# Turning x on the vector engine by block transposes, and splitting the third pair's output projection over idle stretches of the tail

## The chip, the cores and the metric

One Trainium2 chip, one core. The metric is the device time of one execution in microseconds (us). Beside it stands the span of the core, mostly about 1.2 us shorter, which a profile covers. Engines: PE is TensorE (matmul), PEld its weight load, DVE is VectorE, ACT is ScalarE, POOL is GpSimd, SP is SyncE, which here only issues DMA transfers.

## The reference

Two independent problems, A and B, of the same form: one decoding step of attention over a sliding window of a cache. Cut to what matters:

```
# B=2, Sq=1, D=576, Hq=32, Hkv=16, Sk=16384, Dh=128, W=4096, bf16
q = (x @ wq).reshape(B, 1, Hq, Dh)           # x [2,1,576], wq [576,4096]
k, v = k_cache[:, :, -W:], v_cache[:, :, -W:] # each K/V head serves two query heads
p = softmax(q k^T * Dh**-0.5);  o = p v
out = o.reshape(B, 1, Hq*Dh) @ wo             # wo [4096,576]
result = concatenate([A, B], axis=-1)
```

Of the 153 MB that must be read, 134 are K and V. They come as 16 K tiles and 16 V tiles of 4096 KB each, into a ring of four slots; wq (4608 KB per problem) passes through the same ring first.

## The kernel before

The parts that the change and the argument touch; `# ...` marks cuts. Each operation carries its list of dependencies; the order of operations on each engine is the order of the calls. Of the helpers, make_PV multiplies with one V tile, make_evac brings the product out of PSUM, make_dg and make_pick bring it into the form that the output projection reads, and make_projm and make_proj are output projections, with the weight wo.

```python
# The SP queue: wq A, wq B, then the K and V tiles in order.
# wq fills slots 0, 1 and a quarter of slot 2; the first K tile goes to slot 3, the second to slot 0.
slot_of[key] = (n_slot + 3) % NSLOT
first_deps = {0: [q_done[0]], 1: [q_done[0], q_done[1]], 2: [q_done[1]], 3: []}
deps = [last_reader[prior[-1]]] if prior else first_deps[r]     # of the DMA of a tile
# ...
# x: masked copy on DVE, nine PE transposes, two ACT copies, then the projections
d_xs = dve(lambda e: e.tensor_tensor(xs8.rearrange("p (i t) -> p i t", t=2),
                 x8[:, :].unsqueeze(2).broadcast_to([8, D, 2]),
                 hmask[:, 0:2].unsqueeze(1).broadcast_to([8, D, 2]), ALU.mult), [x_dma, d_hm], "xs8")
def f_xT(e, bank):
    bb = bank[:].bitcast(BF16)
    for u in range(NU):                                          # NU = 9
        src = xs8.rearrange("b (c t) -> b t c", t=NU)[:, u, :]
        last = e.transpose(bb[:, 8 * u:8 * u + 8], src, ident_b[0:8, 0:8])
    return last
# ...
q_done[P] = pe(f_q, [wq_dma[P], op_xev], "q%d" % P)              # 36 matmuls for each problem
# ...
# the tail
make_PV(i + 1); make_evac(i + 1)
make_projm(NM - 1)                    # the third pair's projection, 16 steps of two matmuls
make_part(); make_dg(NG - 2); make_pick(NG - 2)
make_rsum(NG - 1); make_pT(NG - 1); make_sums(NG - 1)
make_PV(i + 2); make_evac(i + 2)
make_PV(i + 3, (0,)); make_dg(NG - 1, (0,)); make_pick(NG - 1, (0,))
filler(2)                             # matmuls whose result nobody reads, for the PE clock
make_PV(i + 3, (1, 2)); make_evac(i + 3)
filler(2)
make_dg(NG - 1, (1,)); make_pick(NG - 1, (1,))
make_proj(NG - 2); make_proj(NG - 1); make_E(NPROB - 1)
```

## Time and profile before

| | before |
|---|---|
| time, median of the first 3 runs | 363.27 us (363.23 to 363.83) |
| span of the profiled run | 362.4 us |
| bytes on the one busy DMA queue | 153.1 MB |
| share of the 16 DMA engines' time | 98.5% |

The page of the kernel before, its DMA row in 40 slices (tenths busy) and the queue's line (packets, MB, share of the engines' span):

```profile
span 362.4 us, 2626 instructions
...
DMA  8999999999999999999999999999999999999995
...
q1 hardware_dynamic: 6196, 153.10, 98.5%
```

The DMA engines are busy from the second slice to the last but one. So the kernel's time is the time of the stream, plus a start, plus what follows the last landing.

The timeline of the kernel before between the landing of x and the first projection matmul (columns: start us, duration us, engine, line, operation, tiles, count, and in brackets the idle time before and what ended it):

```profile
15.52 1.35 DVE L217 TENSOR_TENSOR pR<-tmp,hmask 8x1152 bf16<-8x1152 bf16 x1 [13.96 <-DMA tmp<-in_B_x_dram]
...
16.93 0.70 PE L258 MATMUL tb<-ident_b,pR 8*128 8x8 bf16 x9 [16.93 <-DVE pR L217]
...
17.66 0.29 ACT L265 ACTIVATE pT<-tb 128x36 bf16<-128x36 bf16 x2 [12.60 <-PE tb L258]
...
18.09 0.59 PE L279 MATMUL ot<-ring,pT 128*32 128x512 bf16 x1 [0.47 <-ACT pT L265]
```

x lands at 15.5 us and the projection starts at 18.09. The SP engine's DMA issues of the kernel before, from 25 us (the first line merges three K tiles, the second to the fourth; the second K tile's issue is its start):

```profile
27.96 8.95 SPq L377 DMA_DIRECT2D ring<-in_A_k_cache_dram  x3
44.03 0.54 SPq L377 DMA_DIRECT2D ring<-in_A_v_cache_dram  x1
56.13 0.53 SPq L377 DMA_DIRECT2D ring<-in_A_k_cache_dram  x1
```

The second K tile waits for projection A, which reads its slot; it goes out at 27.96 us. The first K tile was issued at 1.73 and took 33.5 us, so it landed at 35.2.

The stretches of the kernel before (stretch and length, busy us of PE, PEld, DVE, ACT, POOL, then granted PE clock, DMA share, GB/s):

```profile
28.00:34.00 6.00, 6.00 (x29) 0.68 (x7) 0.00 (x0) 0.00 (x0) 0.00 (x0) 1.00 1.00 431
34.00:40.00 6.00, 2.70 (x16) 0.67 (x9) 4.77 (x2) 3.00 (x9) 0.00 (x0) 0.92 1.00 431
350.00:356.00 6.00, 4.91 (x29) 1.04 (x20) 1.80 (x4) 0.00 (x0) 0.00 (x0) 0.50 1.00 416
356.00:360.00 4.00, 3.57 (x28) 2.08 (x30) 1.02 (x4) 0.00 (x0) 0.00 (x0) 0.51 0.64 249
```

The stream keeps 431 GB/s through 28 to 40 us. At the end the PE runs at half its clock (granted 0.50 and 0.51 in the last two stretches). The PE's timeline of the tail before:

```profile
352.88 1.90 PE L535 MATMUL ot<-ring,pT 128*32 128x512 bf16 x16 [0.62 <-DMA ring<-in_B_v_cache_dram]
...
357.16 3.45 PE L635 MATMUL pj<-wob,oP 128*2 128x288 bf16 x32
```

The last projection runs 32 matmuls in 3.45 us without a pause and ends at 360.61; the output transfer follows.

### The profile page before, as it was taken

What the parts mean: (1) busy time and instruction counts of PE and PEld (TensorE: products, weight loads), DVE (VectorE), ACT (ScalarE), POOL (GpSimd) and SP (SyncE); (2) the same over time, 40 slices, a digit from 0 to 9 for tenths busy, and PEclk for the clock granted to TensorE, in tenths of its full rate; (3) what the DMA queues carried; (4) which work ended last, traced back from release to release, by engine and by line L of the source; (5) the groups of instructions that cost most, each with busy time, mean ns of one, the idle gap of its engine ahead of it and who ended that gap; (6) DMA issues with size and microseconds to landing.
All of it is one profiled execution on the core that took longest, in us unless ns stands there. A gap on an engine that the chain in (4) does not pass through costs nothing.

```text
span 362.4 us, 2626 instructions
## 1 busy us (share of the span) xinstructions
PE 238.9 (66%) x1294; PEld 58.3 (16%) x935; DVE 211.4 (58%) x141; ACT 46.3 (13%) x80; POOL 22.3 (6%) x83
## 2 busy tenths in 40 slices
PE   0099599556666847662596677557686875666657
PEld 0010111112111201110121121112112120112222
DVE  0201879495949391934909476582917685765532
ACT  1000300040031000400005000500005000501300
POOL 3000101100010001000010000100010001001000
PEclk9999699969897896888888686998688798879976
DMA  8999999999999999999999999999999999999995
GB/s 326 452 427 416 448 418 441 427 430 438 416 447 416 452 416 420 448 423 442 423 436 430 427 434 418 437 441 416 438 429 432 434 434 431 435 423 438 412 415 233
DMA packets 6228, 153.28 MB, mean 423 GB/s; under 512 B 700, under 2 KB 840, under 8 KB 1224
## 3 DMA queue, kind: packets, MB, share of 16 engines
q1 hardware_dynamic: 6196, 153.10, 98.5%
q8 instruction: 9, 0.15, 0.2%
q14 instruction: 3, 0.02, 0.0%
q10 hardware_dynamic: 20, 0.01, 0.0%
HBM read 153.10 MB, written 0.00 MB: 422 GB/s over the span
## 4 chain that ended last, share of the span: by engine, by line
DVE 36%; DMA 28%; PE 23%; issue 8%; ACT 2%; POOL 1%; ACTq 0%; SPq 0%; DVEq 0%; POOLq 0%
DVE xt L432 23%; DMA ring<-in_B_k_cache_dram 16%; DMA ring<-in_B_v_cache_dram 8%; PE st L248 8%; PE st L458 7%; PE pj L248 3%; DMA tmp<-in_B_x_dram 3%; DVE pT L505 3%; DVE oR L564 3%; DVE mx L466 2%; DVE tmp L557 2%; ACT pR L496 1%; PE ot L279 1%; PE pj L616 1%; PE pj L635 1%
## 5 line engine op out<-in xcount | busy, mean ns | idle before, releaser
L458 PE MATMUL st<-xt,zq 128*128 128x512 bf16 x256 | 123.8, 484 | 82.8 <-DVE xt L432 81.4
L432 DVE STREAM_TRANSPOSE xt<-ring 128x4096 f32<-128x4096 f32 x32 | 141.4, 4426 | 27.6 <-DMA ring<-in_A_k_cache_dram 17.0
L248 PE MATMUL st<-xt,zq 128*128 128x512 bf16 x256 | 122.5, 478 | 0.0
L496 ACT ACTIVATE pR<-st,bias 128x512 bf16<-128x512 f32 x32 | 40.1, 1423 | 219.4 <-DVE bias L489 219.4
L458 PEld LDWEIGHTS st<-xt,zq 128*128 128x128 bf16 x256 | 29.3, 114 | 207.0 <-issue 109.4
L535 PE MATMUL ot<-ring,pT 128*32 128x512 bf16 x512 | 32.0, 392 | 8.1 <-DMA ring<-in_B_v_cache_dram 5.6
L489 DVE SCALAR_TENSOR_TENSOR bias<-vmask,tb,offm 128x4 f32<-128x4 f32 x8 | 1.8, 224 | 40.3 <-PE tb L486 40.3
L519 DVE TENSOR_REDUCE ssum<-tb 128x2 f32<-128x8 f32 x8 | 1.3, 161 | 37.4 <-PE tb L516 37.4
L424 POOL TENSOR_TENSOR zq<-qs,bmask 128x64 bf16<-128x64 bf16 x32 | 8.7, 294 | 168.0 <-PE st L248 146.3
L505 DVE STREAM_TRANSPOSE pT<-pR 128x2048 bf16<-128x2048 bf16 x8 | 18.4, 2304 | 0.7 <-ACT pR L496 0.7
L535 PEld LDWEIGHTS ot<-ring,pT 128*32 128x32 bf16 x512 | 12.3, 97 | 22.9 <-DMA ring<-in_B_v_cache_dram 10.6
L557 DVE SCALAR_TENSOR_TENSOR tmp<-ot,rsb,dmask 128x512 f32<-128x512 f32 x16 | 11.5, 718 | 7.7 <-PE ot L535 7.6
L564 DVE TENSOR_REDUCE oR<-tmp 128x128 f32<-128x512 f32 x15 | 15.6, 1043 | 0.5
L248 PE MATMUL pj<-wob,oM 128*2 128x288 bf16 x48 | 11.9, 286 | 0.0
L616 PE MATMUL pj<-wob,oM 128*2 128x288 bf16 x48 | 11.9, 286 | 0.0
L258 PE MATMUL tb<-ident_b,pR 8*128 8x8 bf16 x9 | 0.7, 198 | 16.9 <-DVE pR L217 16.9
L248 PE MATMUL pj<-ring,pT 128*32 128x512 bf16 x36 | 11.7, 409 | 0.0
L466 DVE TENSOR_REDUCE mx<-st 128x2 f32<-128x1024 f32 x8 | 9.7, 1213 | 0.1
L217 DVE TENSOR_TENSOR pR<-tmp,hmask 8x1152 bf16<-8x1152 bf16 x1 | 1.3, 1347 | 14.0 <-DMA tmp<-in_B_x_dram 14.0
L496 ACT ACTIVATION_READ_ACCUMULATOR pR<-st,bias 128x1 f32 x32 | 9.1, 286 | 0.0
L279 PE MATMUL ot<-ring,pT 128*32 128x512 bf16 x18 | 7.5, 419 | 0.5 <-ACT pT L265 0.5
L248 PE MATMUL st<-ring,pT 128*32 128x512 bf16 x18 | 7.3, 407 | 0.0
(69 smaller groups left out, 71.5 us busy)
## 6 DMA issues: line engine op xcount, KB each, us to landing
ring<-in_A_k_cache_dram SPq DMA_DIRECT2D x8, 4096.0 KB, 24.5
ring<-in_A_v_cache_dram SPq DMA_DIRECT2D x8, 4096.0 KB, 29.6
ring<-in_B_k_cache_dram SPq DMA_DIRECT2D x8, 4096.0 KB, 26.6
ring<-in_B_v_cache_dram SPq DMA_DIRECT2D x7, 4096.0 KB, 28.8
ring<-in_A_wq_dram SPq DMA_DIRECT2D x1, 4608.0 KB, 13.8
ring<-in_B_wq_dram SPq DMA_DIRECT2D x1, 4608.0 KB, 24.2
wob<-in_A_wo_dram SPq DMA_DIRECT2D x2, 2304.0 KB, 28.8
wob<-in_B_wo_dram SPq DMA_DIRECT2D x1, 2304.0 KB, 27.5
```

The costliest lines, as they stand in the source:

```text
L248: return e.add_instruction(mybir.InstMatmult(name=nc.get_next_instruction_name(), engine=mybir.EngineType.PE, ins=[e.lower_ap(mv_), e.lowe ...
L279: last = e.matmul(QB[c], wt, mv_, start=first, stop=True, skip_group_check=True)
L424: last = e.tensor_tensor(dst, src, msk, ALU.mult)
L432: Xop[(t, jh)] = dve(lambda e: e.transpose(xt[:, jh, :].bitcast(FP32).rearrange("p (kp x kt) -> p x kp kt", kp=2, kt=2), ring[:, r, jh * H ...
L458: last = e.matmul(ob, wt, mv_, start=first, stop=True, skip_group_check=True)
L466: ch[(G, "max")] = dve(lambda e: e.tensor_reduce(mx[:], st[:, :].rearrange("p (x t) -> p t x", t=2), AX.X, ALU.max), [Sop[(2 * G + 1, 1)]] ...
L496: last = e.activation(pR[:].rearrange("p (x k) -> p k x", k=4)[:, kv, :], st[:, :].rearrange("p (x t) -> p t x", t=2)[:, kv % 2, :], ACTF.Exp,
L505: pT_op[G] = dve(lambda e: e.transpose(pT[:, v, :].rearrange("p (w j q) -> p j w q", w=4, q=8), pR[:].rearrange("p (j w q) -> p j w q", w= ...
L535: last = e.matmul(OTB[32 * c:32 * c + 32, :], pT[:, v, base + 32 * c:base + 32 * c + 32], ring[:, r, jj * 128:(jj + 4) * 128], start=rd == ...
L557: evac_op[i] = dve(lambda e: e.scalar_tensor_tensor(tv, o, rsb[:, v, b:b + 1], dm, ALU.mult, ALU.mult), deps, "ev%d" % i)
L564: ch[(G, "red%d" % b)] = dve(lambda e: e.tensor_reduce(oR[:, b, :], tmp[:].rearrange("p (j d) -> p d j", j=4), AX.X, ALU.add), [evac_op[i] ...
L616: last = e.matmul(PJ[h], oM[:, j, :], mv_, start=start and j == 0, stop=True, skip_group_check=True)
```

## The change

Two independent parts. In the head, x is spread over 32 partitions and turned by eight block transposes on DVE, which takes PE, a PSUM bank and ACT out of the path. In the tail, the third pair's projection is cut in three, with the last four steps and a filler set behind the next-to-last V product, the fillers are longer, and the transfer of the first of the last two wo halves depends only on the projection's first part. The core of the diff, with cuts marked:

```diff
-        x8 = tmp[0:8, 0:D // 2].bitcast(BF16)
-        xs8 = pR[0:8, 0:2 * D]
+        xz = xt[0:32, 0, 0:NPROB * D]
+        xs = xt[0:32, 1, 0:NPROB * 2 * D]
 # ... xz is zeroed by POOL, x is loaded into xz, hmask grows to 32 partitions
+        d_xs = dve(lambda e: e.tensor_tensor(xs.rearrange("p (i t) -> p i t", t=2),
+                                             xz.unsqueeze(2).broadcast_to([32, NPROB * D, 2]),
+                                             hmask[:, 0:2].unsqueeze(1).broadcast_to([32, NPROB * D, 2]), ALU.mult), [x_dma, d_hm], "xs")
+        def f_xT(e):
+            for P in range(NPROB):
+                for k in range(4):
+                    last = e.transpose(xU[32 * k:32 * k + 32, P, :, :],
+                                       xs[:, P * 2 * D:(P + 1) * 2 * D].rearrange("p (c t) -> p t c", t=NU)[:, :, 32 * k:32 * k + 32])
+            return last
 # ... the nine PE transposes and two ACT copies are gone
-            q_done[P] = pe(f_q, [wq_dma[P], op_xev], "q%d" % P)
+            q_done[P] = pe(f_q, [wq_dma[P], d_xT], "q%d" % P)
 # ... tail
-        make_projm(NM - 1)
-        make_part()
+        make_projm(NM - 1, 0, 8)
         make_dg(NG - 2)
+        make_projm(NM - 1, 8, 12)
         make_pick(NG - 2)
 # ...
         make_PV(i + 2)
+        make_projm(NM - 1, 12, 16)
+        filler(4)
+        make_part()
         make_evac(i + 2)
 # ...
-        filler(2)
+        filler(4)
         make_PV(i + 3, (1, 2))
         make_evac(i + 3)
-        filler(2)
+        filler(3)
```

More of the change, by code (lines that the diff above doesn't have):

```diff
@@ L120, in build_kernel @@
         bsel = sb("bsel", [128, 2], FP32)
-        hmask = sb("hmask", [8, 2], FP32)
+        hmask = sb("hmask", [32, 2], FP32)
         mx = sb("mx", [128, 2], FP32)
@@ L178, in f_x @@
                 for h in range(2):
-                    last = e.dma_start(x8[4 * P + 2 * h:4 * P + 2 * h + 2, :], probs[P][0][:, 0, :]).then_inc(x_sem, 16)
+                    last = e.dma_start(xz[4 * P + 2 * h:4 * P + 2 * h + 2, P * D:(P + 1) * D], probs[P][0][:, 0, :]).then_inc(x_sem, 16)
             return last
@@ L199, in build_kernel @@
                                                    base=0, channel_multiplier=1), [p_ones_b], "ident_b")
-        p_zxU = pool(lambda e: e.memset(pTf[:, 0:XW].bitcast(FP32), 0.0), [], "zero_xU")
-        x_dma = dma_op("act", x_sem, 2 * NPROB, f_x, [p_zxU], "x")
+        p_zx = pool(lambda e: e.memset(xz.bitcast(FP32), 0.0), [], "zero_x")
+        x_dma = dma_op("act", x_sem, 2 * NPROB, f_x, [p_zx], "x")
         def f_sel(e):
@@ L215, in mask @@
             return dve(lambda e: e.tensor_reduce(dst, view, axes, ALU.add), [p_ident_f], tag)
-        d_hm = mask(hmask[:, 0:2], ident_f[0:8, 0:8].rearrange("p (g t b) -> p t g b", g=2, t=2), AX.XY, "hmask")
-        d_xs = dve(lambda e: e.tensor_tensor(xs8.rearrange("p (i t) -> p i t", t=2),
-                                             x8[:, :].unsqueeze(2).broadcast_to([8, D, 2]),
-                                             hmask[:, 0:2].unsqueeze(1).broadcast_to([8, D, 2]), ALU.mult), [x_dma, d_hm], "xs8")
+        d_hm = mask(hmask[:, 0:2], ident_f[0:32, 0:32].rearrange("p (g t b) -> p t g b", g=8, t=2), AX.XY, "hmask")
+        d_xs = dve(lambda e: e.tensor_tensor(xs.rearrange("p (i t) -> p i t", t=2),
[7 more added lines that the diff above has]
+            return last
+        d_xT = dve(f_xT, [d_xs], "xT")
         d_bm = mask(bmask[:, 0:4], ident_f[:].rearrange("p (a i) -> p a i", a=4), AX.X, "bmask")
@@ L252, in mm_held @@
                 tile_size=size, tile_position=at))
-        def f_xT(e, bank):
-            bb = bank[:].bitcast(BF16)
-            for u in range(NU):
-                src = xs8.rearrange("b (c t) -> b t c", t=NU)[:, u, :]
-                last = e.transpose(bb[:, 8 * u:8 * u + 8], src, ident_b[0:8, 0:8])
-            return last
-        n_, bank_x, op_xT = tb_job(f_xT, "xT", [d_xs, p_ident_b])
-        def f_xev(e):
-            for P in range(NPROB):
-                src = bank_x[:].bitcast(BF16)[:, 0:NU * 8].rearrange("c (u w) -> c u w", u=NU)[:, :, 4 * P:4 * P + 4]
-                last = e.activation(xU[:, P, :, 4 * P:4 * P + 4], src, ACTF.Copy)
-            return last
-        op_xev = act(f_xev, [op_xT, p_zxU], "xev")
-        tb_consumer[n_] = op_xev
         q_done = {}
@@ L344, in build_kernel @@
         projm_op = {}
+        projm_first = {}
         def issue(key):
@@ L353, in issue @@
                 rows = probs[P][4][gl * 1024:gl * 1024 + 128 * n, :].rearrange("(p j) n -> p j n", j=n)
-                deps = ([projm_op[i - 1]] if i >= 1 else []) if kind == "M" else [projm_op[NM - 1]]
+                deps = ([projm_op[i - 1]] if i >= 1 else []) if kind == "M" else [projm_first[NM - 1] if i == NG - 2 else projm_op[NM - 1]]
                 cuts = [(0, n, wo_sem[i % 2])]
@@ L430, in make_X @@
             r = slot_of[("K", t)]
-            deps = [stream_dma[("K", t)][0][2], Sop[(t - 1, jh)] if t >= 1 else op_xT]
+            deps = [stream_dma[("K", t)][0][2], Sop[(t - 1, jh)] if t >= 1 else d_xT]
             Xop[(t, jh)] = dve(lambda e: e.transpose(
@@ L499, in f @@
                 return last
-            exp_op[G] = act(f, [b4] + prev(G, "rsum8") + ([pT_op[G - 1]] if G >= 1 else [op_xT]), "exp%d" % G)
+            exp_op[G] = act(f, [b4] + prev(G, "rsum8") + ([pT_op[G - 1]] if G >= 1 else []), "exp%d" % G)
         def make_pT(G):
@@ L555, in make_evac @@
             deps = [PVop[i], d_dm, rsb_op[G]]
-            deps.append(ch["tmp"] if i else d_xs)
+            if i:
+                deps.append(ch["tmp"])
             evac_op[i] = dve(lambda e: e.scalar_tensor_tensor(tv, o, rsb[:, v, b:b + 1], dm, ALU.mult, ALU.mult), deps, "ev%d" % i)
@@ L603, in make_pick, with make_projm @@
             ch["tmp"] = ch[(G, "oP", b0)]
-        def make_projm(q):
-            P, start = 2 * q // GP, (2 * q) % GP == 0
+        def make_projm(q, j0=0, j1=16):
+            P, start = 2 * q // GP, (2 * q) % GP == 0 and j0 == 0
             ensure(("M", q))
             def f(e):
-                for j in range(16):
+                for j in range(j0, j1):
                     for h in range(2):
@@ L620, in make_projm @@
                 deps += [e_ops[(P - 1, 0)], e_ops[(P - 1, 1)]] if P >= 1 else [q_ev[2]]
-            projm_op[q] = pe(f, deps, "projm%d" % q)
+            projm_op[q] = pe(f, deps, "projm%d_%d" % (q, j0))
+            if j0 == 0:
+                projm_first[q] = projm_op[q]
         def make_proj(G):
```

## The prediction

> **What bounds the kernel now.** The DMA stream. The page shows one hardware queue with 153.1 MB at 98.5% of the DMA engines' time, in a span of 362.4 us; in the stretches table no 20 us between 40 and 340 us fall below 0.98 of DMA share. Only about 2 us at the start, and what follows the last landing, lie outside. The queue's issue list shows why compute delays between cost nothing: a K or V transfer takes about 10 us, but lands 24 to 31 us after issue, so two to three are queued.
>
> **Head.** x lands at 15.5 us (timeline). Before: masked copy on DVE 1.35 us (8x1152), nine PE transposes 0.7 us, two ACT copies 0.3 us; the first projection matmul starts at 18.09. After: the copy doubles to 2304 elements per partition, 2.7 us; then eight block transposes of 288 elements. The 2048-element bf16 transpose took 2304 ns, so I estimate 0.32 to 0.36 us each, 2.6 to 2.9 us together. The larger memset holds the x DMA back 0.3 us. The first projection matmul starts near 21.4, some 3.3 us later: a loss on the compute chain. The second K tile is issued when projection A ends, 27.9 before, about 31.3 after; the first K tile lands at 35.2, so the queue should not run dry, though the margin shrinks from 7 to 4 us. Tiles 3 and 4 go out at 39 instead of 35.7, with the second landing near 45. Later issues move 3 us, with 10 or more us queued. Cost to the end: 0, at worst 1 us.
>
> **Tail.** The last V piece arrives near 354.1; the two last wo halves land at 356.9 (first) and 358.4, 359.4, 359.9 (three cuts; issue plus time to landing). The granted PE clock is 0.50 from about 350 to 359.8, after PE sat idle 2.8 us before 349.2. The last projection ran without a gap, 32 matmuls in 3.45 us from 357.16, ending 360.6. The change moves four of sixteen projection steps (about 1 us) and a filler of four behind the next-to-last V product (346.4), so that the idle stretch shrinks to about 1 us, and lengthens the later fillers. [...] At full clock the projection takes about 1.9 us and then waits for wo, ending near 360.2. The earlier pick and second transpose (about 1.9 us earlier) gain nothing: the V tile they wait with lands at 344.4. Issuing the first wo half earlier, the second later (about 348), gains nothing: both stand behind V in the queue until 353. Gain: 0.3 to 0.6 us.
>
> **Time.** 363.27 - 0.45 + 0.15 = 363.0 us; 8 in 10: 362.4 to 364.0. Faster by over 2%: 0.01; within 2%: 0.98; slower by over 2%: 0.01.
>
> **What would show it.** Masked copy 2.6 to 2.8 us, eight transposes near 0.35 us each, first projection matmul near 21.4; DMA share unchanged between 20 and 60 us; next-to-last V product still starting at 344.4; granted clock 1.0 from 349 on; waits on wo inside the last projection; its end near 360.2.
>
> **What would make it wrong.** DMA share dropping near 31 to 36 us (the queue ran dry, up to 2 us); cold fillers delaying the last V products past their landing; the longer idle before 344.4 (about 4 us, as projection steps moved away) making that product and its followers late; the late issue of the second wo half moving its landing.

That a shorter idle stretch and longer fillers would keep the clock full was the estimate, from this one trace (granted clock 0.50 after 2.8 us of idle).

## The result, and the profile after

| | before | after |
|---|---|---|
| time, median of 6 runs | 363.74 us (363.23 to 364.07) | 365.01 us (364.77 to 365.61) |
| ratio, 95% interval | | 1.004 (1.0027 to 1.0053) |
| span of the profiled run | 362.4 us | 363.5 us |
| first projection matmul | 18.09 us | 24.10 us |
| second K tile issued | 27.96 us | 33.43 us |

A ratio is the mean time of one kernel's runs over that of the other's of the same rounds, so it is not quite the ratio of the medians. The change costs 1.3 us by the medians (1.5 by the ratio), clear of the noise, where a small gain was forecast and 364.0 was the upper bound.

The timeline of the changed kernel over the same path:

```profile
15.79 2.54 DVE L217 TENSOR_TENSOR xt<-xt,hmask 32x2304 bf16<-32x2304 bf16 x1 [14.21 <-DMA xt<-in_B_x_dram]
18.37 5.59 DVE L224 STREAM_TRANSPOSE pT<-xt 32x288 bf16<-32x288 bf16 x8
...
24.10 0.58 PE L271 MATMUL ot<-ring,pT 128*32 128x512 bf16 x1 [24.10 <-DVE pT L224]
```

The eight transposes took 5.59 us, 0.69 us each, twice the estimate. The projection starts 6.0 us late: 0.3 from x, 1.2 from the copy, and 4.5 because 5.8 us from the copy's end to the first matmul replaced 1.2. The SP engine's issues after:

```profile
33.43 8.96 SPq L370 DMA_DIRECT2D ring<-in_A_k_cache_dram  x3
43.84 0.54 SPq L370 DMA_DIRECT2D ring<-in_A_v_cache_dram  x1
61.36 0.54 SPq L370 DMA_DIRECT2D ring<-in_A_k_cache_dram  x1
```

The second K tile goes out 5.5 us later, still before the first lands at 35.0. The stretches after:

```profile
28.00:34.00 6.00, 6.00 (x30) 0.68 (x7) 0.00 (x0) 0.00 (x0) 0.00 (x0) 1.00 1.00 431
34.00:40.00 6.00, 6.00 (x30) 0.65 (x7) 4.96 (x2) 0.00 (x0) 0.00 (x0) 1.00 0.88 350
350.00:356.00 6.00, 3.32 (x38) 0.98 (x35) 0.68 (x2) 0.00 (x0) 0.00 (x0) 1.00 0.99 414
356.00:360.00 4.00, 2.63 (x25) 1.00 (x19) 2.14 (x5) 0.00 (x0) 0.00 (x0) 1.00 0.89 358
```

The DMA rate drops to 350 GB/s between 34 and 40 us: (431 - 350) x 6 us is 0.49 MB not moved. A narrower stretch shows that the engines stand still:

```profile
33.50:34.70 1.20, 1.20 (x7) 0.10 (x1) 0.00 (x0) 0.00 (x0) 0.00 (x0) 1.00 0.01 0
```

The second K tile was issued at 33.43, and its first packets move only from 34.7. The best single reading is the sum of bytes over time, from the GB/s of consecutive stretches of 8 us (MB up to that time; computed, not a view of its own):

```
us      before   after    behind
 32      12.98   12.98     0.00
 40      16.26   15.73     0.54
 80      33.55   32.98     0.57
160      68.21   67.70     0.50
240     102.65  102.10     0.55
320     137.06  136.48     0.58
```

One step, between 32 and 40 us, and then a constant. On the mean of 168 to 344 us, against the mean of two profiles of the kernel before, the changed kernel is 0.52 MB behind, which at 427 GB/s (taken as the pace of the steady part; the stretches from 48 to 344 us give 430, which would make these losses 1% smaller) is 1.22 us. All of the lost time is lost in the head. The PE in the tail after:

```profile
355.85 0.40 PE L528 MATMUL ot<-ring,pT 128*32 128x512 bf16 x4 [0.45 <-DMA ring<-in_B_v_cache_dram]
...
358.64 1.14 PE L631 MATMUL pj<-wob,oP 128*2 128x288 bf16 x16 [0.27 <-DMA wob<-in_B_wo_dram]
360.12 0.65 PE L631 MATMUL pj<-wob,oP 128*2 128x288 bf16 x8 [0.34 <-DMA wob<-in_B_wo_dram]
361.06 0.66 PE L631 MATMUL pj<-wob,oP 128*2 128x288 bf16 x8 [0.28 <-DMA wob<-in_B_wo_dram]
```

At full clock the projection waits for each cut of wo and ends at 361.7, 5.9 us after the last V product's start (355.85), against 6.5 us in the profile before (the last four matmuls' weights were loaded there at 354.15, the end is 360.61).

### The profile page after: what moved, and what is told of

It reads as the page before. It is cut to its first block, busy times and chain, and to the rows that moved or that the text cites. A ratio compares the mean times of both kernels' runs of the same rounds, so it can differ in the third digit from the quotient of the medians.

```text
span 363.5 us, 2622 instructions
## 1 busy us (share of the span) xinstructions
PE 233.1 (64%) x1292; PEld 56.3 (15%) x927; DVE 218.2 (60%) x149; ACT 46.0 (13%) x78; POOL 22.4 (6%) x83
## 4 chain that ended last, share of the span: by engine, by line
DVE 34%; DMA 32%; PE 22%; issue 8%; ACT 2%; POOL 1%; ACTq 0%; SPq 0%; DVEq 0%; POOLq 0%
DVE xt L425 20%; DMA ring<-in_B_k_cache_dram 16%; DMA ring<-in_B_v_cache_dram 9%; PE st L256 7%; PE st L451 7%; PE pj L256 4%; DMA xt<-in_B_x_dram 3%; DMA wob<-in_B_wo_dram 3%; DVE oR L558 3%; DVE pT L498 2%; DVE mx L459 2%; DVE tmp L551 2%; DVE pT L224 2%; ACT pR L489 1%; PE pj L610 1%
## 5 line engine op out<-in xcount | busy, mean ns | idle before, releaser
L451 PE MATMUL st<-xt,zq 128*128 128x512 bf16 x256 | 121.1, 473 | 83.4 <-DVE xt L425 82.0
L256 PE MATMUL st<-xt,zq 128*128 128x512 bf16 x256 | 119.9, 468 | 0.0
L528 PE MATMUL ot<-ring,pT 128*32 128x512 bf16 x512 | 31.4, 385 | 7.4 <-DMA ring<-in_B_v_cache_dram 7.4
L271 PE MATMUL ot<-ring,pT 128*32 128x512 bf16 x18 | 7.3, 404 | 24.1 <-DVE pT L224 24.1
L512 DVE TENSOR_REDUCE ssum<-tb 128x2 f32<-128x8 f32 x8 | 1.3, 161 | 35.1 <-PE tb L509 35.1
L528 PEld LDWEIGHTS ot<-ring,pT 128*32 128x32 bf16 x512 | 12.1, 97 | 22.3 <-DMA ring<-in_B_v_cache_dram 10.0
L610 PE MATMUL pj<-wob,oM 128*2 128x288 bf16 x48 | 13.0, 304 | 0.0
L256 PE MATMUL pj<-wob,oM 128*2 128x288 bf16 x48 | 12.9, 303 | 0.0
L217 DVE TENSOR_TENSOR xt<-xt,hmask 32x2304 bf16<-32x2304 bf16 x1 | 2.5, 2545 | 14.2 <-DMA xt<-in_B_x_dram 14.2
L271 PEld LDWEIGHTS ot<-ring,pT 128*32 128x32 bf16 x18 | 1.8, 100 | 38.2 <-issue 38.2
```

The lines of the kernel that those rows point to most:

```text
L256: return e.add_instruction(mybir.InstMatmult(name=nc.get_next_instruction_name(), engine=mybir.EngineType.PE, ins=[e.lower_ap(mv_), e.lowe ...
L271: last = e.matmul(QB[c], wt, mv_, start=first, stop=True, skip_group_check=True)
L451: last = e.matmul(ob, wt, mv_, start=first, stop=True, skip_group_check=True)
L528: last = e.matmul(OTB[32 * c:32 * c + 32, :], pT[:, v, base + 32 * c:base + 32 * c + 32], ring[:, r, jj * 128:(jj + 4) * 128], start=rd == ...
L610: last = e.matmul(PJ[h], oM[:, j, :], mv_, start=start and j == 0, stop=True, skip_group_check=True)
```

## The experiments

There were sixteen runs, two of them repeats of the kernels before and after. Theory Q: the loss is the DMA queue running dry, because the second K tile is issued too late. Rivals are named in the expectations. "Behind" is always the mean of 168 to 344 us, as above.

### The two parts of the change alone

`head_only` is the kernel before with only the x part; `tail_only` with only the tail part (the two halves of the diff above).

> Only the x part of the change on the kernel before. Theory H (the head costs, the tail gives back): the eight transposes again take 0.69 us each, the second K tile is issued near 33.4 us, the cumulative DMA bytes fall about 0.5 MB behind between 32 and 36 us, and the time is 363.7 + 1.3 + 0.4 to 0.5 (the tail gain missing) = 365.3 to 365.7 us. Rival T (the rearranged tail costs, by the late issue of the last wo half or the shifted product): the time is that of before, 363.5 to 364.0 us.

> Only the tail part of the change on the kernel before. Theory H: 0.4 to 0.6 us faster than before, near 363.2 us, granted clock near 1 from 349 us on, no step in the cumulative bytes. Rival T: 1 us or more slower than before, near 365 us.

Measured: head alone 365.56 us against 363.43, ratio 1.0037 (1.0014 to 1.0060), transposes 0.69 us each, second K tile issued at 33.90, 0.73 MB behind. Tail alone 363.59 us, ratio 1.0002 (0.9979 to 1.0025), 0.01 MB behind. So the whole loss is the head's, and no harm by the tail is seen. The tail's expected gain of 0.4 to 0.6 us is not seen either; but the interval of its ratio reaches from 0.8 us faster to 0.9 us slower, so the time alone cannot exclude it.

### What makes the transposes slow

`src_contig` reads neighbouring elements (a wrong result); `four_long` turns both problems in one instruction.

```diff
-  xs[:, P*2*D:(P+1)*2*D].rearrange("p (c t) -> p t c", t=NU)[:, :, 32*k:32*k+32]   # changed kernel
+  xs[:, P*2*D:(P+1)*2*D].rearrange("p (t c) -> p t c", t=NU)[:, :, 32*k:32*k+32]   # src_contig
+  xs.rearrange("p (g c t) -> p g t c", g=NPROB, t=NU)[:, :, :, 32*k:32*k+32]       # four_long, k = 0..3
```

> The changed kernel with the eight transposes reading 32 neighbouring elements instead of elements 18 bytes apart; the result is wrong on purpose. If the stride of the read makes them slow (S): 0.32 to 0.38 us each, first projection matmul near 21.4 us, second K tile issued near 31, no step in the bytes, time near 363.2 us. If a fixed cost of an instruction or the 32-partition form makes them slow (F): 0.65 to 0.70 us each still and 365 us.

> The changed kernel with four transposes of 576 elements in place of eight of 288, result correct, same strided read. If the stride sets a cost per element (S): about 1.35 us each, 5.4 us in all, time as the changed kernel, 365 us. If it is a fixed cost of about 0.38 us beside 0.31 us of streaming (F): about 1.0 us each, 4.0 us in all, second K tile issued near 31.9, and most of the lost bytes back: 363.2 to 364.0 us.

The line of the transposes in `src_contig`, from the view of their source line (duration in ns, min/median/max, then first and last start in us):

```profile
L224 DVE STREAM_TRANSPOSE pT<-xt x8: 465/468/471, 18.2 to 21.6; 32x288 bf16<-32x288 bf16 x8
```

The same view of `four_long`:

```profile
L223 DVE STREAM_TRANSPOSE pT<-xt x4: 1203/1203/1210, 18.2 to 21.8; 32x576 bf16<-32x576 bf16 x4
```

Neither pure story fits; both are half right. A later run (`x_near`) gave the fourth point, 768 ns for 576 neighbouring elements. Two straight lines follow. Neighbouring: (768 - 468) / 288 = 1.04 ns an element and 168 ns a piece. Eighteen bytes apart: (1203 - 687) / 288 = 1.79 ns an element and 171 ns a piece. Each line is drawn through two points; for the first there is a third point, the 2048-element transposes of the kernel before: 168 ns + 2048 x 1.04 ns = 2.30 us against 2304 ns. For the second there is none. So of the 2.9 us that the eight exceeded 8 x 0.33, about 1.4 us are the fixed 0.17 us, and 8 x 288 x 0.75 ns = 1.7 us the stride, less 0.2 us of the fixed part that the forecast's rate already held. The forecast had scaled a 2048-element transpose, in which the fixed part hides.

Only one stride was run (18 bytes: 1.79 against 1.04 ns an element), so what about it makes the reads slow is not shown; nor is what the fixed 0.17 us consists of.

Times: `src_contig` 364.21 us, 1.0014 (0.9989 to 1.0038), 0.19 MB behind; `four_long` 364.43, 1.0018 (0.9996 to 1.0040), 0.21 MB behind. Both lie between before and after. A caution: `src_contig` was accepted as correct although x was scrambled, so the comparison with the reference says little about q here; the rearrangement of `x_near` below was checked against the original by working out the indices, and agrees.

### How long a delay is free

`delay14`, `delay22` and `delay36` are the kernel before with idle reductions put into the x path; `before_again` is the kernel before against itself.

```diff
+        def f_delay(e):
+            for i_ in range(14):                    # or 22, 36
+                last = e.tensor_reduce(scr[:, i_:i_ + 1], ident_f[:], AX.X, ALU.add)
+            return last
+        d_delay = dve(f_delay, [p_ident_f, d_xs], "delay")
-        n_, bank_x, op_xT = tb_job(f_xT, "xT", [d_xs, p_ident_b])
+        n_, bank_x, op_xT = tb_job(f_xT, "xT", [d_delay, p_ident_b])
```

> The kernel before with 14 idle vector reductions (0.19 us each) put between the masked copy and the transposes of x: projection 2.7 us later, second K tile issued near 30.6 to 31.7 us. This is the delay that the prediction expected of the change. Theory Q (the queue runs dry once the second K tile is issued less than about 3 us before the first lands at 35.2 us; from there each us costs a us): 0 to 0.2 us over before. Rival C (the delay runs through the compute chain to the end): 2.7 us over before.

> The same with 22 reductions: 4.2 us later, second K tile issued near 32.1 to 33.2. Theory Q: 0.2 to 1.2 us over before, and a step in the cumulative bytes at 32 to 40 us that then stays constant. Rival C: 4.2 us.

> The same with 36 reductions: 6.9 us later, issue near 34.8 to 35.9. Theory Q: 2.7 to 3.7 us over before, a step of 1.1 to 1.6 MB. Rival C: 6.9 us. If the queue needs no lead at all (as the prediction took it): 0 to 0.7 us.

> The kernel before, unchanged, against itself. Gives the noise: ratio 1.000 within 0.002. Its profile gives a second look at the granted clock of the last projection: if half clock there is not fixed (as the changed tail alone, where the clock fell again, lets one think), the end of the last projection after the last V piece varies between 5.9 and 6.5 us from run to run; if it is fixed, it is 6.4 again.

Measured ratios: 1.0032 (1.0006 to 1.0058), 1.0030 (1.0014 to 1.0046), 1.0083 (1.0065 to 1.0100), and 1.0014 (1.0001 to 1.0026) for the unchanged kernel. So a difference of 0.15% is not to be read from these times, and the bytes are the better measure. Two expectations were missed: `delay14` took about 1.2 us (0.2 to 2.1) more instead of at most 0.2, while its bytes show 0.43 us; and the step of `delay36` is 0.93 MB, or 2.2 us, instead of 1.1 to 1.6 MB, though its time fits (the profiled execution was the fastest of its six). Rival C, the whole delay reaching the end, is out: 7 us of delay cost 3. So is a queue that needs no lead.

All profiles in which the second K tile waits for projection A, in the order of its issue (the reference is the mean of `before`, issue at 27.96, and `before_again`):

```
kernel          second K tile issued   behind at 168-344 us    in us (/0.427)
before_again            27.64               0.00                  0.00
tail_only               29.03              -0.01                  0.0
delay14                 31.18               0.18                  0.43
src_contig              31.96               0.19                  0.46
delay22                 32.22               0.35                  0.82
four_long               32.54               0.21                  0.49
after                   33.43               0.52                  1.22
x_near                  33.65               0.64                  1.50
head_only               33.90               0.73                  1.71
after_again             34.22               0.86                  2.01
delay36                 34.39               0.93                  2.18
```

From 33.4 on, issue minus loss is 32.2 each time (33.43 - 1.22 = 32.21, 34.39 - 2.18 = 32.21): from 32.2 on, every microsecond of delay is a microsecond of the stream. Between 31 and 32.6 there is a soft edge of up to 0.8 us. The first K tile lands near 35.1, so the queue must have its next transfer about 2.9 us before the landing. In bytes: wq and the first K tile are 13.6 MB, and by the sums above they are through at about 33.5 us, 1.3 us after the edge. The prediction had taken the landing itself as the deadline.

The traces show both parts of this lead. In the kernel before, the 2 us from 33.5 are busy:

```profile
33.50:35.50 2.00, 2.00 (x11) 0.19 (x2) 0.27 (x1) 0.00 (x0) 0.00 (x0) 1.00 0.99 426
```

In `delay36` the same stretch is empty:

```profile
33.50:35.50 2.00, 2.00 (x11) 0.19 (x2) 0.62 (x1) 0.00 (x0) 0.00 (x0) 1.00 0.00 0
```

Where the queue was empty, the first packets moved 1.3 us after the start of the issue, which itself takes 0.54 us (33.43 to 34.7 in `after`, 34.22 to 35.5 in `after_again`, 34.39 to 35.7 in `delay36`, in stretches of 0.1 us). So 33.5 - 1.3 = 32.2 is the edge. The other 1.6 us, from 33.5 to the landing at 35.1, pass after the last bytes have moved. What makes the edge soft is open.

### Yardstick, and a repair on the vector engine that failed

`after_again` is the changed kernel once more; `x_near` writes the masked copy so that four long transposes read neighbours.

```diff
+  for t in range(2):                               # x_near: eight small multiplications
+      for eo in range(2):
+          us = [u for u in range(NU) if (u + NU * eo) % 2 == t]
+          # ... for each problem P
+          last = e.tensor_scalar(xo[:, P, us[0]:us[-1]+1:2, :, eo].rearrange("p u c -> p c u"),
+                                 xi[:, P, :, a0:a0+n], hmask[:, t:t+1], None, ALU.mult)
```

> The changed kernel with the masked copy written so that the transposes read neighbouring elements, and four transposes of 576 in place of eight of 288, result correct. From the two transpose runs (0.17 us an instruction plus 1.03 ns an element when near): 0.76 us each, 3.05 us in all in place of 5.5. The masked copy becomes eight small multiplications by a column, together 1.5 to 3 us. First projection matmul at 20.3 to 21.8 us, second K tile issued near 30 to 31.5, bytes at most 0.2 MB behind, span 362.0 to 362.8 us.

> The changed kernel, unchanged, on the chip of these runs, as the yardstick: 1.2 to 1.6 us over before, second K tile issued near 33.4, about 0.5 MB behind.

Measured: `after_again` 1.0034 (1.0019 to 1.0048). Its second K tile went out at 34.22 and not at 33.4, though its projection began earlier (23.85): the same 36 matmuls took 10.4 us instead of 9.3. In all profiles this took 9.3 to 10.9 us. The difference is the number of slow first matmuls: about 7 in `after` and about 12 in `after_again` (ten up to 28 us in its timeline, the rest from the 10.4 us) start 0.43 us apart, the others 0.22 us, though the granted clock in the record of `after` is 1.00 from 24 to 28 us. Why the number varies is not shown; here it moves the loss between 1.2 and 2.0 us. `x_near` was a miss: 1.0046 (1.0032 to 1.0060). The transposes took 0.77 us each as expected, but the copy became slow, 5.32 us instead of 2.54; that its scattered writes did it is the guess (not tested apart). Its DVE timeline:

```profile
15.45 5.32 DVE L225 TENSOR_SCALAR xt<-xt,hmask 32x320 bf16<-32x320 bf16 x8 [13.87 <-DMA xt<-in_B_x_dram]
20.80 3.11 DVE L232 STREAM_TRANSPOSE pT<-xt 32x576 bf16<-32x576 bf16 x4
```

The stride had been moved from the reads of one operation to the writes of another.

### Taking the wait away, with the slow transposes in place

If Q is right, the slow head must cost nothing once the second K tile no longer waits for it. Three attempts. `early_k1` puts the second K tile into slot 2, three quarters of which are free from the start; its last quarter follows the third tile. `early_k1_act` issues that quarter on the scalar engine's queue, and `early_four` adds the four long transposes.

```diff
-  slot_of[key] = (n_slot + 3) % NSLOT
+  slot_of[key] = (2, 0, 1, 3)[(n_slot + 3) % NSLOT]
+  stream[1:3] = [("A", 1), ("K", 2), ("K", 1)]     # early_k1: A is the upper three quarters, without a wait
+  stream[1:3] = [("A", 1), ("K", 1), ("K", 2)]     # early_k1_act: the quarter K1 goes out on the ACT queue
```

> The changed kernel, slow transposes kept, but three quarters of the second K tile go to a part of the ring that the projection weights do not use, so they are issued right behind the first K tile and wait for no projection; the last quarter follows the third tile. Theory Q (all of the loss is the DMA queue that runs dry for want of the second K tile): no step in the cumulative bytes at 32 to 40 us (below 0.1 MB), span 362.0 to 362.6 us, within 0.5 us of before, though the first projection matmul still starts at 24.1 us. Rival C (the late projection costs by itself): span 363.5 us or more as the changed kernel.

> As the run with the early second K tile, but its last quarter is issued on the scalar engine's queue, in place of behind the third tile, so that it no longer holds the compute chain back. In the earlier run the sixth K tile was issued at 90.8 us, and the bytes queued ahead of it (38.8 MB) were through at 92.0 us at the pace of before: lead 1.2 us. Theory Q2 (the same lead rule bites a second time, at the sixth K tile): issue near 88.8 to 89.9, lead 2.1 to 3.2 us, bytes at most 0.3 MB behind after 100 us in place of 0.5, span 362.3 to 363.0 us. Rival (moving the second tile costs in itself, or the late projection does): 0.5 MB behind and 363.5 us again.

> The same with the four long transposes, projection 0.7 to 0.9 us earlier. Theory Q2: sixth K tile issued near 88.0 to 89.0 us, lead 3 us or more, no step anywhere above 0.1 MB, span 362.0 to 362.5 us, that of before, with the first projection matmul still 5 us late. Rival: above 363 us.

`early_k1`: 365.00 us, 1.0040 (1.0027 to 1.0052); by the time, Q had lost. By the bytes it had not: the step at 32 to 40 us was gone (0.03 MB behind at 56 to 88 us), but 0.46 MB were lost at 92 to 104 us. At that place a second deadline waits. The sixth K tile's slot is freed by the compute chain; before, it was issued at 83.52, here at 90.79, and the 38.8 MB queued ahead of it were through at 92.0.

`early_k1_act` and `early_four` missed badly: 372.96 and 372.13 us, 1.0267 and 1.0235. The quarter (1 MB) went out at 46.26 on the ACT queue and was there only when the transpose of the second tile could start, at 62.84; that held the chain, and the sixth K tile, back. Lines of `early_k1_act`, from the timeline:

```profile
46.26 0.61 ACTq L376 DMA_DIRECT2D ring<-in_A_k_cache_dram  x1
...
62.84 8.77 DVE L431 STREAM_TRANSPOSE xt<-ring 128x4096 f32<-128x4096 f32 x2 [18.91 <-DMA ring<-in_A_k_cache_dram]
...
100.35 0.54 SPq L376 DMA_DIRECT2D ring<-in_A_k_cache_dram  x1
```

The ACT queue moved its bytes slowly while both queues were at work: between 54 and 58 us the SP queue (q1) and the ACT queue (q10) moved nearly the same number of packets, 44 and 43, but 1.44 and 0.35 MB (packets, MB, share of the engines' time). So the 1 MB landed only 16.6 us after its issue (46.26 to 62.84), during which the SP queue moved 6.1 MB.

```profile
q1 hardware_dynamic: 44, 1.44, 83.9%
q10 hardware_dynamic: 43, 0.35, 20.9%
```

As a repair it is useless, as a measurement it is a strong one: issue at 100.35, 4.18 MB or 9.79 us behind; 100.35 - 9.79 = 90.6, the same edge as `early_k1` shows (90.79 - 1.09 = 89.7) within a microsecond. The first packets moved at 101.6, again 1.3 us after the issue. (1.1 MB of the loss were there by 88 us already: an earlier tile, issued at 82.91, was late too. What is lost earlier does not change the difference of issue and loss.) The expected lead of 2 to 3 us for this kernel was wrong, because I had not reckoned with the slow landing.

`free_slot` puts the last two blocks of wq B (1 MB) into the buffer of wo, unused until 118 us, so that slot 2 is free from the start; the second K tile is issued at once and whole (slots in the order of `early_k1`). `free_four` adds the four long transposes, `free_before` does the same to the kernel before.

```diff
+  wq_end = wob[:].rearrange("p j n -> p (j n)")[:, 0:LW]         # LW = two blocks
+  e.dma_start(ringf[:, QW:2 * QW - LW], src[:, 0:QW - LW]).then_inc(wq_sem[P], 16)
+  return e.dma_start(wq_end, src[:, QW - LW:QW]).then_inc(wq_sem[P], 16)
-  first_deps = {0: [q_done[0]], 1: [q_done[0], q_done[1]], 2: [q_done[1]], 3: []}
+  first_deps = {0: [q_done[0]], 1: [q_done[0], q_done[1]], 2: [], 3: []}   # second K tile: slot 2
```

> The changed kernel, slow transposes kept, with the last two blocks of the second projection weight put in the still unused buffer of the output weights, so that the second K tile has a free ring slot and is issued at once, whole, before x has even landed. Nothing is held back on the compute chain. Theory Q2: no step at 32 to 40 us; sixth K tile issued near 88.8 to 89.9 us against 92.0 for the end of the bytes ahead of it, lead 2.1 to 3.2 us, so 0 to 0.3 MB behind after 100 us; span 362.0 to 362.9 us. Rival (late projection or slow transposes cost by themselves): 0.5 MB behind, span above 363.4 us.

> The same with four long transposes (0.85 us less delay). Theory Q2: lead of the sixth K tile 3 us or more, no step above 0.1 MB anywhere, span 361.9 to 362.5 us, within 0.5 us of before.

> The kernel before with the same free slot and the second K tile issued at once. The queue never ran dry before, so theory Q2 expects nothing: within 0.4 us of before. If earlier issue gains by itself, 0.5 us or more faster.

| kernel | ratio to before | first projection matmul | sixth K tile issued | behind |
|---|---|---|---|---|
| `free_slot` | 1.0007 (0.9989 to 1.0025) | 23.57 | 89.99 | 0.12 MB, 0.29 us |
| `free_four` | 0.9997 (0.9985 to 1.0009) | 22.75 | 88.77 | 0.07 MB, 0.17 us |
| `free_before` | 1.0008 (0.9995 to 1.0022) | 17.93 | 84.70 | 0.03 MB, 0.06 us |

With the slow transposes still there and the projection still 5.5 us late, the changed kernel is back at the time of before. The stretch in which the changed kernel had lost its bytes is full again in `free_slot` (437 GB/s, before 431, changed kernel 350):

```profile
34.00:40.00 6.00, 6.00 (x29) 0.68 (x7) 4.74 (x2) 0.00 (x0) 0.00 (x0) 1.00 1.01 437
```

That settles the cause. The first projection matmul in the timeline of `free_four`:

```profile
22.75 0.58 PE L277 MATMUL ot<-ring,pT 128*32 128x512 bf16 x1 [22.75 <-DVE pT L228]
```

And the issue of its sixth K tile, from the SP engine's timeline:

```profile
88.77 0.54 SPq L376 DMA_DIRECT2D ring<-in_A_k_cache_dram  x1
```

And `free_before` shows that issuing earlier than the edge gains nothing. No version was found that is clearly faster than the kernel before.

### Where the tail's gain went

`before_again` answers that. Its stretches at the end (columns as above; the third number from the right is the granted clock):

```profile
350.00:356.00 6.00, 3.64 (x37) 1.13 (x36) 3.27 (x7) 0.00 (x0) 0.00 (x0) 1.00 0.99 409
356.00:360.00 4.00, 2.74 (x34) 1.45 (x34) 0.96 (x3) 0.00 (x0) 0.00 (x0) 1.00 0.62 245
```

The PE's timeline of its last V piece and last projection:

```profile
354.30 0.40 PE L535 MATMUL ot<-ring,pT 128*32 128x512 bf16 x4 [0.45 <-DMA ring<-in_B_v_cache_dram]
...
357.08 1.14 PE L635 MATMUL pj<-wob,oP 128*2 128x288 bf16 x16 [0.26 <-DMA wob<-in_B_wo_dram]
358.57 0.66 PE L635 MATMUL pj<-wob,oP 128*2 128x288 bf16 x8 [0.34 <-DMA wob<-in_B_wo_dram]
359.55 0.65 PE L635 MATMUL pj<-wob,oP 128*2 128x288 bf16 x8 [0.32 <-DMA wob<-in_B_wo_dram]
```

The same kernel, at full clock, waiting for wo, ending 5.9 us after the last V piece: exactly the tail that the change was to bring. The half clock in the first profile was that execution's, not the kernel's. Of seven profiles with the old tail the last projection ran at full clock in five. The new tail is no guarantee either: in the profile of `tail_only` the clock fell to 0.50 within the last projection and it ended at 360.6, as in the first profile of before. There the PE's longest pause since 350 us was 0.9 us, against 2.8 us of idle before the fall in `before`; what makes the clock fall is not shown. Whether the new tail makes the full clock more frequent (all but one of its profiles had it) these runs can't say; in the time it gains nothing that could be measured. As an estimate: at half clock the old tail ended 6.5 us (before) and 6.9 us (`head_only`) after the last V product instead of 5.9, but only in two profiles of seven, which is 0.2 us on the mean, less than these runs resolve.

## Why the prediction was right or wrong

- **Bound.** "The DMA stream": right. Every loss clear of the noise is a step in the bytes moved.
- **Masked copy 2.7 us, x 0.3 us later.** Right in size: 2.54 and 0.27 (in other profiles x came without delay).
- **"I estimate 0.32 to 0.36 us each, 2.6 to 2.9 us together."** This is the step that failed: 0.69 us each, 5.59 together. The estimate scaled a long transpose by elements and left out the fixed 0.17 us of a piece and the 18-byte stride. With 2.8 us in their place the second K tile would, as an estimate (33.43 less 2.8), have gone out near 30.6, before the edge (in a profile whose 36 matmuls take 9.3 us; with the 10.9 us also seen, at it).
- **"The first K tile lands at 35.2, so the queue should not run dry, though the margin shrinks from 7 to 4 us."** The mechanism was named, and named again among what would make it wrong, but the deadline was wrong: it is 32.2, so the margin was 4.2 us to begin with (32.2 - 27.96). Even the issue that was forecast, 31.3, leaves only 0.9 us, and in `delay14`, at 31.18, 0.43 us were lost.
- **"Later issues move 3 us, with 10 or more us queued."** Too generous: at the sixth K tile (83.52) the bytes ahead last to 92.0, and the edge is near 90. It did not matter in the changed kernel, whose stream was already late; it did in `early_k1`.
- **Tail, gain 0.3 to 0.6 us.** Not seen: 1.0002, though its interval (0.9979 to 1.0025) does not exclude it. The geometry was right (at full clock the projection waits for wo and ends 0.5 us sooner). What failed is the premise: that the kernel before always runs it at half clock was read from one execution, and five of seven profiles show full clock.
- **Re-ordered wo transfers and earlier pick: nothing.** Not contradicted: the whole tail part together changed nothing (1.0002); they were not run apart.

In the sum 363.27 - 0.45 + 0.15, the 0.45 measured about 0 (within 0.9 us either way), and the 0.15 measured 1.2 to 2.0.

## What to carry to other kernels

In a kernel bound by its DMA stream, give every early compute step the latest time at which a transfer that waits for it may be issued, and count that back from the end of the bytes ahead of it, with the lead measured here of 1.3 to 2.5 us (one for one from 1.3, first losses from 2.5), not from the landing. Cost a short block transpose on the vector engine as a fixed part plus elements at the rate of its own stride (here 0.17 us, and 1.04 ns an element for neighbours or 1.79 ns at 18 bytes), and don't scale down a long one. Before building on a clock or a pause in a tail, look at a second profile of the same kernel (here the last projection ran at half clock in two profiles of seven).
